# Top-k attention and an MLP mixer in one kernel: q of the first pair split, output sums by two chunks, stores on two queues, and new scheduling weights

## The chip, the core and the metric

The kernel runs on one core of one Trainium2 chip. The core has five engines that run side by side and wait for each other by semaphores: TensorE (PE in the profile; its weight loads are PEld), VectorE (DVE), ScalarE (ACT), GpSimd (POOL) and SyncE (SP, used here to issue DMA transfers). Sixteen DMA engines move data between the chip's memory (HBM) and the on-chip SBUF; TensorE writes its results into PSUM. The metric is the device time of one execution in microseconds, lower is better.

## The reference

Eight batches, eight heads, 576 rows, head dimension 64. For each row of the scores the 32 largest are kept, the others are masked, and the softmax of what is kept weighs v. The heads are put side by side (512 channels) and go through a mixer: an MLP over the rows (576 to 256 to 576) with a residual, then an MLP over the channels (512 to 1536 to 512) with a residual.

```python
scores = scale * np.matmul(q, k.transpose(0, 1, 3, 2))
kth = np.partition(scores, -top_k, axis=-1)[..., -top_k:-top_k + 1]     # top_k = 32
scores = np.where(scores >= kth, scores, -1000000000.0)
attn = np.exp(scores - np.max(scores, axis=-1, keepdims=True))
attn = attn / (np.sum(attn, axis=-1, keepdims=True) + 1e-09)
x = heads_side_by_side(np.matmul(attn, v))                              # [8, 576, 512]
xt = x.transpose(0, 2, 1)
u = x + (np.maximum(xt @ w_tok1, 0.0) @ w_tok2).transpose(0, 2, 1)
out = u + np.maximum(u @ w_ch1, 0.0) @ w_ch2
```

## The kernel before

Work is done in 32 pairs of heads. A pair has nine units of 128 score rows: groups g = 0 to 3 with two units each (one of each head) and g = 4 with one unit, which holds the last 64 rows of both heads. For a unit, TensorE makes the scores, ScalarE copies them to SBUF (`S`, L472), VectorE finds the 8 largest of each of seven segments (L479), and from these an upper threshold `thi`; ScalarE counts and signs what lies above (`sg`, L493), GpSimd multiplies that with the scores (`X`, L496), and VectorE finds the exact threshold `tlo` in the product (L508). Then the masked exponentials `Pm` are made in one of four forms, named by a letter for each g:

```python
FORMS = ("DRADR", "QQADR", "DRQDD", "RQADR")            # by pair % 4
FIRST = ("QRDRD", "RQRQR", "QQRRQ", "DRRQR")            # pairs 0 to 3
LAST = ("DQADA", "AAAAD")                               # pairs 30 and 31
# D: ScalarE exp; GpSimd: nt, Z (one per unit), M, then Pm = E * M
# R: ScalarE makes the mask (L534), TensorE adds it to recomputed scores, ScalarE exp
# Q: as R, but GpSimd makes the mask (nt, Z, M)
# A: ScalarE exp into PSUM (L565), VectorE compares and multiplies (L568)
```

`Pm` is transposed by DMA (in the last pair's g = 3 and 4 by TensorE), and TensorE multiplies it with v; VectorE normalises (L455, L456). After four pairs a batch's mixer follows.

The kernel does not fix the order of instructions by hand. It adds every operation to a plan with an engine, an estimated length and a due time, and a list scheduler in Python puts them in order once: among what can run, the earliest possible start is taken first, and nearly equal starts are settled by the due time. The due times come from a table of weights:

```python
W = dict(T=2.1, ev=-7.1, evh=5.45, seg=10.8, t2=3.2, ct=2.3, xm=3.05, dm=3.5, m5=-3.85, ...)
...
pick = earliest start; within 0.03 us of each other: smallest (due, number)
```

Loading and transposing q and k of a pair (`cp` is a ScalarE copy out of PSUM with a scale):

```python
def ld_q():
    ld_main(qL, q, nc.sync)                       # two DMAs: rows 0 to 511 of each head
    for h in range(2):
        nc.sync.dma_start(out=qL.t[64*h : 64*h+ST, 4, h, :], in_=q[b, h0+h, SM:S, :])
...
lq = plan.add("SP", 0.24, tl, ld_q, acq=[qL], dma=1.4)
lk = plan.add("SP", 0.2, tl + 0.1, ld_kv(kL, k, keng), acq=[kL], dma=1.4)     # keng: ScalarE's queue in pair 0
oq = plan.add("PE", 0.75, tt, tr(pq, qL, 5), [lq], acq=[pq, qT], use=[qL])     # five transposes, L385
ok = plan.add("PE", 0.75, tt + 0.5*T, tr(pk, kL, 4), [lk], acq=[pk, kT], use=[kL])
eq = plan.add("ACT", 0.6, tt + T, cp(qT, pq, 5*P), [oq], use=[pq, qT])         # L395
ek = plan.add("ACT", 0.57, tt + 1.5*T, cp(kT, pk, S), [ok], use=[pk, kT])
...
om = plan.add("PE", 1.3 if g < 4 else 1.2, T*i0, scores ..., [eq, ek], acq=bs + [Ss], use=[qT, kT])   # L414, L406
```

PSUM is four tiles `big` of two halves each; a half alone is a `one`. The last batch has a mixer of its own. Three of its four channel blocks (`NC - 1`) are done ahead, as partial hidden products (L737) that ScalarE copies to SBUF (L749, `ready`). When the last block of UT is there (L658), a loop over the 12 inner chunks `fc` (`NF`) finishes them:

```python
r1 = plan.add("PE", 1.8, d - 0.5, lambda: residual(range(NC - 1)), uts[0 : NC-1] + l4, acq=outs, use=[UT])   # L764; outs: three big
for fc in range(NF):
    for u in range(2):                            # two halves of 288 rows
        pb = Buf("one")
        o = plan.add("PE", 0.16, ..., hidden(... last block ...), uts + [ready[fc]], acq=[pb], ...)          # L737
        adds.append(plan.add("DVE", 0.42, ..., part(fc) = pb + part(fc), [o, ready[fc]], ...))               # L787
    if fc == 0:
        prev = plan.add("PE", 0.4, ..., residual((NC - 1,)), uts + [r1], ...)
    relus.append(plan.add("ACT", 0.57, ..., relu of part(fc) into H2, adds, ...))                             # L792
    if fc < NF - 2:
        def f(fc=fc):
            for t in range(5):
                outer(t, fc)                      # H2 chunk times wc2b into output block t, L769
        prev = plan.add("PE", 1.12, d + 2.0, f, [relus[-1], prev], use=[H2] + outs)
for t in range(5):
    ...                                           # the last two chunks, then the copy out of PSUM (L808)
    plan.add("SP", 0.06, ..., lambda: nc.sync.dma_start(out=out[...], in_=ob...), [e], use=[ob], dma=1.0)     # L811
```

Of the kernel before, what the change touches and what calls it, by code (L numbers as in the profile page):

```python
# [8 lines left out]
P = 128  # L9
# [3 lines left out]
HUP = float(2.0**20)  # L13
# [15 lines left out]
NEG = -float(2.0**120)  # L29
BIG = float(2.0**60)  # L30

# [178 lines left out]
def kernel(  # L210
# [11 lines left out]
    nc = tc.nc  # L222
# [3 lines left out]
    AF = mybir.ActivationFunctionType  # L226
# [10 lines left out]
    SM = 512  # L237
# [81 lines left out]
    for t in qLs:  # L319
        nc.vector.memset(t[:, 4, :, :], 0.0)  # L320
    for t in vLs:
        nc.vector.memset(t[:, 4, :, :], 0.0)
    for t in Xs:
# [13 lines left out]
    def flat(t):  # L337
        return t[:, :, :].rearrange("p j c -> p (j c)")
# [4 lines left out]
    def pair_ops(p):  # L343
# [7 lines left out]
        def ld_main(buf, src, eng):  # L351
            for h in range(2):
# [2 lines left out]
                    in_=src[b, h0 + h, 0:SM, :].rearrange("(p t) d -> p t d", t=4),  # L355
                )

        def ld_q():
            ld_main(qL, q, nc.sync)
            for h in range(2):  # L360
                nc.sync.dma_start(
                    out=qL.t[64 * h : 64 * h + ST, 4, h, :], in_=q[b, h0 + h, SM:S, :]
                )

        def ld_kv(buf, src, eng):
            def f():
# [14 lines left out]
        def tr(dst, src, n):  # L381
            def f():
                o = flat(dst.t)
                for t in range(n):
                    nc.tensor.transpose(o[:, t * P : (t + 1) * P], src.t[:, t, :, :], identF[:, :])  # L385
                if n == 4:
# [7 lines left out]
        def cp(dst, src, n):  # L394
            return lambda: nc.scalar.activation(  # L395
                out=dst.t[:, 0:n], in_=flat(src.t)[:, 0:n], func=AF.Copy, scale=HUP)

        eq = plan.add("ACT", 0.6, tt + T, cp(qT, pq, 5 * P), [oq], use=[pq, qT])
        ek = plan.add("ACT", 0.57, tt + 1.5 * T, cp(kT, pk, S), [ok], use=[pk, kT])
# [20 lines left out]
        for g in range(5):  # L420
            n = 2 if g < 4 else 1
            bs, Ss = [Buf("big") for _ in range(n)], Buf("S")
            i0 = 9 * p + 2 * g
            om = plan.add("PE", 1.3 if g < 4 else 1.2, T * i0, lambda g=g, bs=bs: scores(g, bs, True), [eq, ek], acq=bs + [Ss], use=[qT, kT])
            PT.append(unit_ops(i0, n, bs, Ss, om, p, g, scores, [qT, kT]))


# [286 lines left out]
    def mlp_tail(b, base, UT, H2, uts):  # L714
# [44 lines left out]
        def residual(ccs):  # L759
            for t in range(5):  # L760
                for cc in ccs:

                    w = C if cc == 0 else P
                    nc.tensor.matmul(  # L764
                        out=acc(t, cc * P, cc * P + w), lhsT=UT.t[:, cc, t * P : t * P + rows[t]],
                        rhs=identW[:, 0:w], start=(cc == 0), stop=False, skip_group_check=True)
# [4 lines left out]
                start=False, stop=(fc == NF - 1), skip_group_check=True)  # L771

        d = base + 4 * 1.3
        r1 = plan.add("PE", 1.8, d - 0.5, lambda: residual(range(NC - 1)), uts[0 : NC - 1] + l4, acq=outs, use=[UT])
        relus = []
        prev = None
        for fc in range(NF):
            B_, half = parts[fc]
            d += 1.4
            adds = []  # L780
            for u in range(2):
                pb = Buf("one")
# [4 lines left out]
                adds.append(plan.add("DVE", 0.42, d + 0.3 + 0.4 * u, lambda fc=fc, pb=pb, us=us: nc.vector.tensor_tensor(  # L787
                    out=part(fc)[:, us], in0=pb.t[:, pb.half, 0:HS], in1=part(fc)[:, us], op=ALU.add),
                    [o, ready[fc]], use=[pb, B_]))
            if fc == 0:  # L790
                prev = plan.add("PE", 0.4, d + 0.5, lambda: residual((NC - 1,)), uts + [r1], use=[UT] + outs)
            relus.append(plan.add("ACT", 0.57, d + 1.2, lambda fc=fc: nc.scalar.activation(  # L792
                out=H2.t[:, fc, :], in_=part(fc), func=AF.Relu), adds, use=[B_, H2]))
            if fc < NF - 2:
                def f(fc=fc):
                    for t in range(5):
                        outer(t, fc)

                prev = plan.add("PE", 1.12, d + 2.0, f, [relus[-1], prev], use=[H2] + outs)
        for t in range(5):  # L800
            def f(t=t):
                for fc in (NF - 2, NF - 1):
                    outer(t, fc)

            prev = plan.add("PE", 0.45, d + 2.5 + 0.1 * t, f, [prev] + relus[NF - 2 :], use=[H2] + outs)
# [5 lines left out]
            plan.add("SP", 0.06, d + 4 + 0.1 * t, lambda t=t, ob=ob: nc.sync.dma_start(  # L811
                out=out[b, t * P : t * P + rows[t], :], in_=ob.t[0 : rows[t], t % 2, 0:C]), [e], use=[ob], dma=1.0)


# [59 lines left out]
    c2 = plan.add("PE", 0.2, tc_ + 9, lambda: nc.tensor.matmul(  # L874
        out=pb.t[0:1, 0, 0:1], lhsT=ones[:, :], rhs=bad[:, 3:4], start=True, stop=True), [c1], acq=[pb])
    c3 = plan.add("DVE", 0.15, tc_ + 10, lambda: nc.vector.tensor_copy(out=flag[:, :], in_=pb.t[0:1, 0, 0:1]),
                  [c2], use=[pb], lat=3.0)
    plan.add("SP", 1.0, tc_ + 11, lambda: found.append(
        nc.values_load(flag[0:1, 0:1], min_val=0, max_val=P * (NT + 2))), [c3])
# [181 lines left out]
```

## Time and profile before

| | |
|---|---|
| time, median of 3 runs | 832.36 us (831.48 to 832.98) |
| span of the profiled execution | 830.7 us |
| granted TensorE clock, mean | 0.977 of full speed |
| busiest engine by line | VectorE: L479 404.2 us, L508 220.5 us, L483 98.1 us, L482 97.7 us |
| first scan on VectorE | 12.09 us |
| last store issued | 823.52 us |
| HBM read, written | 35.85 MB, 9.44 MB |

An engine's busy time as a share of the span says how full it is over the whole; a table of windows says when. The chain that ended last is followed back from the last instruction, at each step to what released it; an item on that chain delays the end, one beside it does not. In the timeline an item has its start, its length, engine and line, what it writes and reads, and in brackets the engine's idle time before it and what ended it. Times are in microseconds.

### The profile page before, as it was taken

Reading aid. Unit: us, or ns where it says so; the run is one execution under the profiler, and the core shown is the slowest. Engines: PE = TensorE matmul, PEld = TensorE weight load, DVE = VectorE, ACT = ScalarE, POOL = GpSimd, SP = SyncE. Lnnn points to the kernel's source line nnn. Section 1 sums busy time; section 2 is a strip of 40 time slices with the busy share of each in tenths; the row PEclk is TensorE's granted clock in tenths of the full one; section 3 lists DMA queues with packets and bytes.
Section 4 is the critical chain, followed back from the end, with each engine's and each line's share of the span. In section 5 each row is a group of like instructions: output and inputs, shape, how many; then the busy total and the mean of one; then the engine's idle time right before and its main releaser. Section 6 shows DMA issues by size and latency. Waiting matters only on the chain.

```text
span 830.7 us, 20132 instructions
## 1 busy us (share of the span) xinstructions
PE 735.4 (89%) x5744; PEld 464.6 (56%) x5783; DVE 787.7 (95%) x4794; ACT 753.1 (91%) x1468; POOL 691.4 (83%) x560
## 2 busy tenths in 40 slices
PE   5778778899989989899989999899989999898994
PEld 3445455665556555665556555565556655574641
DVE  5999999999999999999999999999999999999853
ACT  6899998999999999999999999999999999997732
POOL 1999887899899988899988998899989999998400
PEclk9799999999999999999999999999999999999998
DMA  5986955547645565437646466445565385234301
GB/s 128 148 150 118 168 119 99 101 77 155 134 90 96 111 134 113 97 80 147 137 88 115 82 151 117 99 99 122 129 107 109 72 150 126 44 69 92 80 1 61
DMA packets 311064, 89.62 MB, mean 108 GB/s; under 512 B 303776, under 2 KB 305696, under 8 KB 310944
## 3 DMA queue, kind: packets, MB, share of 16 engines
q1 hardware_dynamic: 306992, 84.19, 51.0%
q0 software_dynamic: 2752, 3.77, 3.1%
q8 instruction: 47, 0.77, 0.4%
q14 instruction: 73, 0.60, 0.2%
q10 hardware_dynamic: 1200, 0.30, 0.2%
HBM read 35.85 MB, written 9.44 MB: 55 GB/s over the span
## 4 chain that ended last, share of the span: by engine, by line
DVE 73%; PE 10%; ACT 8%; issue 4%; POOL 2%; DMA 1%; SPq 0%; DVEq 0%; ACTq 0%; POOLq 0%
DVE cd L479 28%; DVE tlo L508 18%; DVE cd L483 9%; DVE m L482 5%; DVE X L504 3%; DVE thi L490 3%; PE big L414 3%; DVE Pm L568 3%; DVE Xb L456 2%; ACT S L472 2%; ACT sg L493 2%; PE big L769 1%; PE big L624 1%; POOL X L496 1%; PE big L737 1%
## 5 line engine op out<-in xcount | busy, mean ns | idle before, releaser
L479 DVE MAX8 cd<-S 128x8 f32<-128x82 f32 (+1 forms) x2016 | 404.2, 231 | 8.9 <-ACT S L472 8.9
L496 POOL TENSOR_TENSOR X<-S,sg 128x1152 f32<-128x1152 f32 (+1 forms) x160 | 343.8, 2161 | 46.2 <-ACT sg L493 45.5
L414 PE MATMUL big<-kT,qT 64*128 64x288 f32 x1504 | 255.4, 439 | 13.0 <-ACT kT L395 11.5
L493 ACT ACTIVATE sg<-S,thi 128x576 bf16<-128x576 f32 x288 | 232.0, 807 | 16.6 <-DVE thi L490 12.0
L508 DVE MAX8 tlo<-X 128x8 f32<-128x588 f32 x288 | 220.5, 766 | 1.4 <-POOL nt L518 0.9
L414 PEld LDWEIGHTS big<-kT,qT 64*128 64x128 f32 x1504 | 151.0, 192 | 83.2 <-issue 21.6
L472 ACT COPY S<-big 128x576 f32<-128x576 f32 x288 | 177.9, 670 | 5.1 <-PE big L414 3.7
L527 POOL TENSOR_TENSOR Pm<-E,M 128x1152 bf16<-128x1152 bf16 (+1 forms) x51 | 112.1, 2198 | 4.3
L669 PE MATMUL big<-UT,wc1b 128*128 128x288 bf16 x672 | 95.1, 286 | 19.7 <-ACT Pm L560 7.7
L689 PE MATMUL big<-wc2b,H 128*128 128x512 bf16 (+1 forms) x399 | 97.9, 379 | 5.7 <-issue 1.9
L483 DVE MATCH_REPLACE8 cd<-m,cd 128x14 f32<-128x14 f32 (+1 forms) x576 | 98.1, 171 | 0.0
L482 DVE MAX8 m<-cd 128x8 f32<-128x14 f32 (+1 forms) x576 | 97.7, 170 | 0.0
L560 ACT ACTIVATE Pm<-big 128x576 bf16<-128x576 f32 x143 | 88.4, 674 | 6.8 <-PE big L414 4.8
L669 PEld LDWEIGHTS <-wc1b 128*128 128x128 bf16 x672 | 63.0, 97 | 53.3 <-issue 37.6
L521 POOL TENSOR_SCALAR Z<-S,nt 128x576 f32<-128x576 f32 x94 | 70.3, 748 | 8.8
L554 PE MATMUL big<-M,sink 128*128 128x288 bf16 x286 | 53.5, 293 | 18.8 <-ACT M L534 5.6
L406 PE MATMUL big<-kT,qT 128*128 128x288 f32 x220 | 66.8, 427 | 3.7 <-ACT S L472 1.4
L689 PEld LDWEIGHTS <-H 128*128 128x128 bf16 (+1 forms) x420 | 39.2, 100 | 50.1 <-issue 13.4
L493 ACT ACTIVATION_READ_ACCUMULATOR sg<-S,thi 128x1 f32 x288 | 64.9, 225 | 0.0
L437 PEld LDWEIGHTS <-PT 128*128 128x128 bf16 x1600 | 52.3, 98 | 14.3 <-issue 9.2
L437 PE MATMUL big<-vb,PT 128*128 128x65 bf16 x1600 | 56.0, 194 | 4.3 <-DMA PT<-Pm 2.5
L534 ACT ACTIVATE M<-S,tlo 128x576 bf16<-128x576 f32 x76 | 56.4, 784 | 2.7 <-DVE tlo L508 2.4
(109 smaller groups left out, 1042.5 us busy)
## 6 DMA issues: line engine op xcount, KB each, us to landing
qL<-in_q_dram SPq DMA_DIRECT2D x64, 128.0 KB, 2.8
vL<-in_v_dram SPq DMA_DIRECT2D x64, 128.0 KB, 2.8
kL<-in_k_dram SPq DMA_DIRECT2D x62, 128.0 KB, 2.8
out_dram<-ob SPq DMA_DIRECT2D x14, 512.0 KB, 3.0
PT<-Pm SPq DMA_TRANSPOSE x158, 3.4
wc1b<-in_moe_w_ch_dram POOLq DMA_DIRECT2D x4, 384.0 KB, 6.1
wc2b<-in_moe_w_ch_dram POOLq DMA_DIRECT2D x4, 384.0 KB, 5.8
qL<-in_q_dram SPq DMA_DIRECT2D x64, 16.0 KB, 2.3
```

Source lines behind the costliest of these rows:

```text
L414: nc.tensor.matmul(out=row(bs[h].t)[:, lo:hi], lhsT=qT.t[r, g * P : (g + 1) * P], rhs=kT.t[r, lo:hi], start=start, stop=True,)
L437: nc.tensor.matmul(out=o[:, g, :], lhsT=src[:, (5 * h if g < 4 else 0) + j, :], rhs=vb.t[:, j, h, :], start=(j == 0), stop=(j == 4),)
L472: evs = [plan.add("ACT", 0.525, t + W["ev"] * T + W["evh"] * h * T, lambda h=h: nc.scalar.copy(out=S_.t[:, h, :], in_=row(s[h].t)), [om], ...
L479: segs = [plan.add("DVE", 0.148, th + W["seg"] * T + 0.01 * a, lambda a=a, cd=cd, h=h: nc.vector.max(cd.t[:, a, :], S_.t[:, h, bounds[a] : ...
L482: m_ = lambda n_, cd=cd, m8=m8: (lambda: nc.vector.max(m8.t[:, :], cd.t[:, :, 0:n_]))
L483: c_ = lambda n_, cd=cd, m8=m8: (lambda: nc.vector.match_replace(cd.t[:, :, 0:n_], m8.t[:, :], cd.t[:, :, 0:n_], NEG))
L493: cts.append(plan.add("ACT", 0.77, th + W["ct"] * T, lambda h=h, i=i, r=r: nc.scalar.activation(out=sg.t[:, h, :], in_=S_.t[:, h, :], func ...
L496: xm = plan.add("POOL", 0.1 + 1.19 * n, te + W["xm"] * T, lambda: nc.gpsimd.tensor_tensor(out=X.t[:, XW - S : XW - S + n * S].rearrange("p ...
L508: m = plan.add("DVE", 0.682, te + W["m5"] * T + 0.3 * h * T, lambda h=h, r=r: nc.vector.max(tlo[:, r : r + 8], X.t[:, h * XW : (h + 1) * X ...
L527: last = [plan.add("POOL", 0.12 + 1.11 * n, te + W["pm"] * T, lambda: nc.gpsimd.tensor_tensor(out=Pm.t[:, 0:n, 0:S], in0=E.t[:, 0:n, :], i ...
L669: nc.tensor.matmul(out=row(pb.t)[:, lo:hi], lhsT=wc1b[:, cc, fc * P : (fc + 1) * P], rhs=UT.t[:, cc, lo:hi], start=(cc == 0), stop=(cc == ...
L689: nc.tensor.matmul(out=pb.t[0:r, pb.half, :], lhsT=H2.t[:, fc, cs], rhs=wc2b[:, fc, :], start=(fc == 0), stop=False)
```

## The change

Four things change in the code, and with them the weights of the plan and the forms of four pairs.

In the first pair the last chunk of q (the rows from 512 on) is loaded, transposed and copied as operations of their own, which only the scores of g = 4 wait for; k is copied out of PSUM by VectorE; the memset of `qL` comes first. In the last mixer the loop's output products are taken for two inner chunks at a time, and the first residual products wait for the partial hidden products. The five last stores alternate between SyncE's and ScalarE's queues. The final check of the kernel takes half a PSUM tile instead of a whole one. It is meant to let the scores start sooner, to leave the scheduler better orders, and to shorten the end.

```diff
 W = dict(
-    T=2.1, ev=-7.1, evh=5.45, seg=10.8, t2=3.2, ct=2.3, xm=3.05, dm=3.5, m5=-3.85, ex=9.2, tn=-1.5,
-    z=5.3, mk=-1.2, pm=-2.7, rw=-3.9, og=7.85, eg=7.95, ea=3.15, st=7.0, tr=-0.45, pv=7.5, fin=-9.5,
-    mlp=11.1, stp=1.35, mlq=13.6, stq=1.2, hp=2.85, hps=5.15,
+    T=2.0, ev=-8.45, evh=7.05, seg=3.9, t2=4.5, ct=1.7, xm=3.35, dm=-8.15, m5=-11.15, ex=11.0,
+    tn=-9.4, z=5.9, mk=-11.4, pm=2.35, rw=-0.8, og=6.5, eg=7.6, ea=2.3, st=7.25, tr=-0.35, pv=1.95,
+    fin=3.55, mlp=10.8, stp=1.35, mlq=22.9, stq=0.55, hp=-1.5, hps=0.0,
 )
-FIRST = ("QRDRD", "RQRQR", "QQRRQ", "DRRQR")
-LAST = ("DQADA", "AAAAD")
+FIRST = ("QRDRD", "RQRQR", "QRRQQ", "RRRQQ")
+LAST = ("DRADD", "DAADA")
...
+    for t in qLs:                                  # moved to the front from further down
+        nc.vector.memset(t[:, 4, :, :], 0.0)
     make_identity(nc, identF[:, :])
...
-        lq = plan.add("SP", 0.24, tl, ld_q, acq=[qL], dma=1.4)
+        first = p == 0
+        lq2 = None
+        if first:
+            lq = plan.add("SP", 0.2, tl, lambda: ld_main(qL, q, nc.sync), acq=[qL], dma=1.4)
+            lq2 = plan.add("SP", 0.2, tl + 0.05, lambda: ld_rest(nc.sync), use=[qL], dma=0.2)
+        else:
+            lq = plan.add("SP", 0.24, tl, ld_q, acq=[qL], dma=1.4)
...
-        oq = plan.add("PE", 0.75, tt, tr(pq, qL, 5), [lq], acq=[pq, qT], use=[qL])
+        oq = plan.add("PE", 0.75, tt, tr(pq, qL, 4 if first else 5, True), [lq], acq=[pq, qT], use=[qL])
...
+        if first:
+            eq = plan.add("ACT", 0.5, tt + T, cp(qT, pq, SM), [oq], use=[pq, qT])
+            ek = plan.add("DVE", 0.67, tt + T, lambda: nc.vector.tensor_scalar(
+                out=kT.t[:, :], in0=flat(pk.t)[:, 0:S], scalar1=HUP, scalar2=None, op0=ALU.mult), [ok], use=[pk, kT])
+            o4 = plan.add("PE", 0.2, tt + T, tr(pq, qL, 5, True, 4), [lq2, oq], use=[qL, pq])
+            eq4 = plan.add("ACT", 0.2, tt + 1.5 * T, cp(qT, pq, 5 * P, SM), [o4], use=[pq, qT])
...
-        r1 = plan.add("PE", 1.8, d - 0.5, lambda: residual(range(NC - 1)), uts[0 : NC - 1] + l4, acq=outs, use=[UT])
+        r1 = plan.add("PE", 1.8, d - 0.5, lambda: residual(range(NC - 1)), uts[0 : NC - 1] + l4 + ready, acq=outs, use=[UT])
...
-            if fc < NF - 2:
+            if fc == 1 or (fc > 1 and fc % 2 and fc < NF - 2):
                 def f(fc=fc):
                     for t in range(5):
-                        outer(t, fc)
-                prev = plan.add("PE", 1.12, d + 2.0, f, [relus[-1], prev], use=[H2] + outs)
+                        for c in (fc - 1, fc):
+                            outer(t, c)
+                prev = plan.add("PE", 2.4, d + 2.0, f, [relus[-2], relus[-1], prev], use=[H2] + outs)
...
-            plan.add("SP", 0.06, d + 4 + 0.1 * t, lambda t=t, ob=ob: nc.sync.dma_start(
+            q_ = nc.sync if t % 2 == 0 else nc.scalar
+            plan.add("SP" if t % 2 == 0 else "ACT", 0.6, d + 4 + 0.1 * t, lambda t=t, ob=ob, q_=q_: q_.dma_start(
...
-    pb = Buf("big")                                # the final check's PSUM
+    pb = Buf("one")
```

More of the change, by code (lines that the diff above doesn't have):

```diff
@@ L318 @@
         nc.vector.memset(kdum[:, j : j + 1], float(2 * (j + 1) - 529))
-    for t in qLs:
-        nc.vector.memset(t[:, 4, :, :], 0.0)
     for t in vLs:
@@ L356, in ld_main, with ld_rest @@
                 )
+        def ld_rest(eng):
+            for h in range(2):
+                eng.dma_start(
+                    out=qL.t[64 * h : 64 * h + ST, 4, h, :], in_=q[b, h0 + h, SM:S, :]
+                )
         def ld_q():
             ld_main(qL, q, nc.sync)
[L360 to L363, printed above, removed]
+            ld_rest(nc.sync)
         def ld_kv(buf, src, eng):
@@ L379, in pair_ops, with tr @@
         pq, pk = Buf("big"), Buf("big")
-        def tr(dst, src, n):
+        def tr(dst, src, n, isq=False, lo=0):
             def f():
                 o = flat(dst.t)
-                for t in range(n):
+                for t in range(lo, n):
                     nc.tensor.transpose(o[:, t * P : (t + 1) * P], src.t[:, t, :, :], identF[:, :])
-                if n == 4:
+                if not isq:
                     nc.tensor.transpose(o[:, SM:S], src.t[0:ST, 4, :, :], identF[0:ST, 0:ST])
@@ L390, in pair_ops, with cp @@
         tt = t0 - W["tr"] * T
[L391 removed]
+        oq = plan.add("PE", 0.75, tt, tr(pq, qL, 4 if first else 5, True), [lq], acq=[pq, qT], use=[qL])
         ok = plan.add("PE", 0.75, tt + 0.5 * T, tr(pk, kL, 4), [lk], acq=[pk, kT], use=[kL])
[L394 removed]
+        def cp(dst, src, n, lo=0):
             return lambda: nc.scalar.activation(
[L396 to L399 removed]
+                out=dst.t[:, lo:n], in_=flat(src.t)[:, lo:n], func=AF.Copy, scale=HUP)
+        eq4 = None
+        if first:
[4 more added lines that the diff above has]
+            eq4 = plan.add("ACT", 0.2, tt + 1.5 * T, cp(qT, pq, 5 * P, SM), [o4], use=[pq, qT])
+        else:
+            eq = plan.add("ACT", 0.6, tt + T, cp(qT, pq, 5 * P), [oq], use=[pq, qT])
+            ek = plan.add("ACT", 0.57, tt + 1.5 * T, cp(kT, pk, S), [ok], use=[pk, kT])
         ov = plan.add("ACT", 0.6, t0 + 4 * T, lambda: nc.scalar.copy(
@@ L423, in pair_ops @@
             i0 = 9 * p + 2 * g
-            om = plan.add("PE", 1.3 if g < 4 else 1.2, T * i0, lambda g=g, bs=bs: scores(g, bs, True), [eq, ek], acq=bs + [Ss], use=[qT, kT])
+            om = plan.add("PE", 1.3 if g < 4 else 1.2, T * i0, lambda g=g, bs=bs: scores(g, bs, True), [eq, ek] + ([eq4] if g == 4 else []),
+                          acq=bs + [Ss], use=[qT, kT])
             PT.append(unit_ops(i0, n, bs, Ss, om, p, g, scores, [qT, kT]))
@@ L874 @@
     c2 = plan.add("PE", 0.2, tc_ + 9, lambda: nc.tensor.matmul(
-        out=pb.t[0:1, 0, 0:1], lhsT=ones[:, :], rhs=bad[:, 3:4], start=True, stop=True), [c1], acq=[pb])
-    c3 = plan.add("DVE", 0.15, tc_ + 10, lambda: nc.vector.tensor_copy(out=flag[:, :], in_=pb.t[0:1, 0, 0:1]),
+        out=pb.t[0:1, pb.half, 0:1], lhsT=ones[:, :], rhs=bad[:, 3:4], start=True, stop=True), [c1], acq=[pb])
+    c3 = plan.add("DVE", 0.15, tc_ + 10, lambda: nc.vector.tensor_copy(out=flag[:, :], in_=pb.t[0:1, pb.half, 0:1]),
                   [c2], use=[pb], lat=3.0)
```

## The prediction

> **What bounds the kernel now.** I read, in this order: the page's busy shares, the table of windows, the chain of waits at the start, the timeline of the last 50 us, and the last stores. First, which engine is full, on the page:
>
> ```profile
> PE 735.4 (89%) x5744; PEld 464.6 (56%) x5783; DVE 787.7 (95%) x4794; ACT 753.1 (91%) x1468; POOL 691.4 (83%) x560
> ```
>
> VectorE (DVE) is busy 787.7 of 830.7 us. Its 43 idle us are not spread out. The table of windows (us of the stretch, then busy time of each engine, granted clock, DMA share, GB/s) shows where they lie:
>
> ```profile
> 0.00:12.10 12.10, 6.39 (x31) 4.86 (x31) 2.02 (x29) 4.02 (x6) 0.70 (x6) 1.00 0.56 127
> 200.00:400.00 200.00, 186.61 (x1463) 118.17 (x1472) 199.15 (x1231) 192.01 (x376) 182.93 (x147) 1.00 0.57 114
> ...
> 790.00:819.00 29.00, 25.39 (x135) 10.65 (x136) 14.89 (x39) 11.12 (x18) 0.00 (x0) 0.94 0.00 1
> 819.00:831.00 12.00, 1.73 (x8) 0.47 (x6) 1.99 (x3) 1.17 (x2) 0.00 (x0) 0.68 0.31 106
> ```
>
> In the middle VectorE lacks 0.85 us in 200. The idle time is 10.1 us ahead of the first scan, 14.1 us in the last MLP, 10.0 us in the stores and the end. The windows from 12.1 to 710 us together hold only about 4 us of it, the one from 710 to 790 about 5 us. So new priorities can win at most some 4 us in the long middle; the rest must come from the two ends or from less VectorE work.
>
> The chain at the start (start, length, what):
>
> ```profile
> 1.50 4.08 DMA qL<-in_q_dram
> 5.71 2.15 PE big L385 x9
> 8.16 1.26 PE big L385 x5
> 9.42 2.02 PE big L414 x8
> ...
> 12.09 1.27 DVE cd L479 x8
> ```
>
> The q transfer that released TensorE was issued at 1.50, which is the second main piece, not the last chunk (those issues start at 2.40). Nine transposes follow, one more for k, then five for the next pair at 8.16, which stand in TensorE's order before the first scores.
>
> The end, from the timeline (start, length, engine, line, output<-input, idle before):
>
> ```profile
> 784.65 0.19 POOL L518 TENSOR_SCALAR nt<-tlo 128x1 f32<-128x1 f32 x1 [1.87 <-DVE tlo L508]
> 786.52 1.28 POOL L527 TENSOR_TENSOR Pm<-E,M 128x576 bf16<-128x576 bf16 x1
> 789.95 0.82 DVE L456 TENSOR_TENSOR Xb<-big,rd 128x640 bf16<-128x640 f32 x1
> 793.43 1.93 PE L764 MATMUL big<-identW,UT 128*128 128x512 bf16 x15
> 793.54 0.64 ACT L658 CAST UT<-big 128x576 bf16<-128x576 f32 x1 [0.44 <-PE big L652]
> ...
> 808.26 1.37 PE L769 MATMUL big<-wc2b,H 128*128 128x512 bf16 x5
> 809.56 0.42 PE L737 MATMUL big<-UT,wc1b 128*128 128x288 bf16 x2
> 810.02 0.82 DVE L787 TENSOR_TENSOR E<-big,E 128x288 f32<-128x288 f32 x2 [1.04 <-PE big L737]
> 810.93 0.68 ACT L792 ACTIVATE H<-E 128x576 bf16<-128x576 f32 x1 [1.18 <-DVE E L787]
> 811.67 1.37 PE L769 MATMUL big<-wc2b,H 128*128 128x512 bf16 x5
> ```
>
> The last attention unit has form D: its mask runs on GpSimd (POOL) for 3.15 us, 784.65 to 787.80, while VectorE mostly waits. Then come the last MLP and its loop over 12 inner chunks: hidden product, two additions, ReLU, five output products. The loop takes 3.41 us for two chunks (808.26 to 811.67): it is a closed round of waits, 2.11 us from a hidden product to its output product and 1.30 us of output products.
>
> [...] The trace has 0.692 us for 512 columns[...], so I take 0.76 us for the k copy. [...] the seven at 818.50 took 1.70 us, 243 ns each[...] and I use 243.
>
> **Part 1, the start.** Splitting q frees the first four transposes from the last chunk, but the main piece landed last by the chain, so this gives at most 0.1 us. By the kernel's scheduling rule (earliest possible start first) the fifth q transpose still goes ahead of k's, because in its model q's remainder lands before k. So k is transposed at 8.17 as before. ScalarE stood idle for 0.45 us just before its k copy (0.65 us), so VectorE's 0.76 us copy wins nothing by itself. Moving the memset of qL up spends 0.3 us that VectorE has free. The next pair's five transposes (1.26 us) may or may not still stand ahead of the scores; kT is ready near 8.9 and the scores start at 9.4, so 0.5 us is at stake. I count **0.2 us less**.
>
> **Part 2, other forms for early and late pairs.** An A unit costs VectorE one operation of 805 ns (40.4 us for 51). The late pairs go from 3 + 8 A units to 2 + 5: four fewer, 4 x 0.805 = 3.2 us less VectorE work. The early pairs have no A in either version. A D unit instead costs POOL about 0.10 + 0.75 + 0.58 + 1.19 = 2.6 us (half of 193, 1147 and 2369 ns, and 748). The late pairs go from five D units to nine: 10.5 us more, less 2.8 us for one Q pair that becomes R. POOL was idle 6.23 + 4.63 + 1.87 = 12.7 us in 766 to 785, so it has room. The very last unit becomes A: 0.85 us of VectorE in place of 3.15 us of POOL. But the unit pair before it becomes D, with 0.19 + 1.5 + 1.15 + 2.37 = 5.2 us, with 0.2 us of hops, after its thresholds. These were known at 783.2 before; earlier by 3.4 us (parts 1 and 2) they are known near 779.8, so that chain ends near 785.2; ten transposes (0.8), a copy (0.82), PV (0.5) and norm (1.1) add 3.2 us: 788.4 against 790.8. **2.4 us less** remains of 3.2.
>
> **Part 3, the order in the last MLP.** The residual products (L764, 1.93 us) now wait for all partial hidden products, whose priority is lower and equal. Before, they ran from 793.43 to 795.29 and held up the first hidden product, though the last UT copy ended at 794.18. If they now run while VectorE normalises, 1.1 us goes: **1.0 us less**. Taking two chunks at a time makes ten output products, 10 x 0.243 = 2.43 us in one piece, and removes no product. Only one PSUM buffer (two halves) is left for the hidden products. By the same rule I read the order as: output of two chunks, then the second half of the next odd chunk, addition, ReLU, output. That round is 2.43 + 1.69 = 4.12 us for two chunks, more than 3.41. But it starts with output products about 2.9 us after the first hidden product, has four such rounds, and ends at 2.9 + 4 x 4.12 + 2.43 + 1.7 = 23.5 us, against 818.50 - 795.29 = 23.2 before, since the loop before lost time in its first chunks. **0.3 us more.**
>
> **Part 4, the stores.**
>
> ```profile
> L811 SPq DMA_DIRECT2D out_dram<-ob x4: 356/394/613, 820.1 to 821.9; - x4
> L811 SPq DMA_DIRECT2D out_dram<-Z x1: 482/482/482, 823.5 to 823.5; - x1
> ```
>
> The fifth store was issued at 823.52, though its copy ended at 821.53 and the fourth issue at about 822.3; the first store's landing, up to 3.4 us after 820.07, fits that wait. With three stores on one queue and two on the other it can issue near 821.7. The data keep the DMA engines busy until about 824.5 either way. I take **1.7 us less** of the 1.8 at most.
>
> **Part 5, all priorities.** T and 26 weights change the order on all engines over 700 us. At most about 4 us are to be won; ScalarE and TensorE are so full that an unlucky order loses as much. I take **0.3 us less** with 2 us either way.
>
> Sum: -0.2 - 2.4 - 1.0 + 0.3 - 1.7 - 0.3 = -5.3; 832.36 - 5.3 = **827.0 us**.
>
> **Rivals.** (a) POOL becomes the bound at the end: pairs 30 and 31 then hold 18 units of scaling (about 1.2 us each) and nine D units, 45 us in two pairs that take about 49. For it: POOL was 90% busy from 12 to 740 us and its operations stay in order. Against it: the idle 12.7 us. It would give back the 2.4 us and perhaps 2 more: 829 to 832. (b) The two-chunk loop runs at 4.12 us in every round and loses the good start: 3 to 4 us more, 830 to 831. Or the other way: if both halves of the next odd chunk stand ahead of the output products, ReLU hides behind them and the round falls to about 3.0 us: 2 to 4 us less, 823 to 825. (c) The new priorities make a recurring bubble in the middle, such as a wait of 0.5 us per pair: 31 x 0.5 = 15 us more. Nothing in the change points to one, but no view of the old trace can exclude it; a search over the weights that kept the better ones speaks against it.
>
> **Range and chances.** The independent parts spread by about 2 us (end), 2 us (loop), 2 us (middle) and 1 us (start and stores): together about 3.7, so 8 in 10 gives 821.5 to 832.5. Two per cent is 16.6 us; faster by that would need almost half of all idle time of VectorE, slower by that needs (c). I give 0.02 and 0.02, and 0.96 to within 2%.
>
> **What would show it.** First scan at 11.5 to 12.1; VectorE's form A at 47 instead of 51, its busy total near 785; last norm ending near 788; no residual products between the last UT copy and the first hidden product; about 4.1 us from one ten-product group to the next; last store issued within 1 us of its copy. Wrong if the stretch from 12 to 780 us changes by over 2 us, if POOL has no idle time in the last pairs, or if the loop's round is near 3.0 us.

## The result, and the profile after

The changed kernel takes 838.36 us, median of four runs (836.39 to 840.53), against 832.67 us (831.48 to 833.45) for the kernel before beside it: a ratio of 1.007 with a 95% interval of 1.0041 to 1.01. It is about 5.7 us slower. The prediction was 827.0 us with a range that ended at 832.5: the sign was wrong and the time lies above the range. The profiled execution is the shortest of the four, with a span of 834.6 us against 830.7 before, so the two traces show 3.9 us of the 5.7.

The busy shares of the page say that the engines' work came out much as expected:

```profile
PE 739.3 (89%) x5756; PEld 465.6 (56%) x5795; DVE 785.7 (94%) x4791; ACT 754.0 (90%) x1470; POOL 695.0 (83%) x564
```

VectorE does 2.0 us less work than before (785.7 against 787.7) and the span is longer: the loss is waiting time. The table of windows of the changed kernel, with the same columns as before (us of the stretch, busy time of PE, PEld, DVE, ACT, POOL, granted clock, DMA share, GB/s), shows where:

```profile
0.00:12.10 12.10, 6.26 (x29) 4.87 (x31) 2.78 (x29) 3.11 (x5) 0.70 (x6) 1.00 0.56 125
200.00:400.00 200.00, 188.31 (x1466) 118.20 (x1474) 199.46 (x1227) 191.76 (x377) 182.72 (x147) 1.00 0.59 113
790.00:819.00 29.00, 20.56 (x110) 9.09 (x111) 13.11 (x34) 9.19 (x15) 0.00 (x0) 0.94 0.00 1
819.00:834.00 15.00, 5.14 (x23) 1.93 (x23) 3.28 (x7) 2.54 (x4) 0.00 (x0) 0.89 0.25 84
```

At the start nothing changed in size. From 200 to 400 us VectorE is busier by 0.3 us; from 12.1 to 200 us, not in the table, it is less busy by 1.3 us (184.44 of 187.90 us against 185.74). From 790 to 819 TensorE is busy 20.6 us where it was 25.4, and 5.1 us of its work has slid into the last window, where it had 1.7. The last MLP has become slower, and the marks of the two profiled executions put a number on it:

| us from the start | before | after |
|---|---|---|
| first scan on VectorE | 12.09 | 12.41 |
| last norm ends | 790.77 | 789.84 |
| last UT copy ends | 794.18 | 793.25 |
| first hidden product of the loop | 795.29 | 794.37 |
| output products of the last two chunks start | 818.50 | 823.53 |
| last store issued | 823.52 | 826.98 |
| span | 830.7 | 834.6 |

The loop over the inner chunks takes 823.53 - 794.37 = 29.2 us where it took 23.2: **6.0 us more**. The stretch before it is 0.9 us shorter and the end after it (834.6 - 823.53 = 11.1 against 12.2) 1.1 us shorter. That is the whole difference of the traces: 6.0 - 0.9 - 1.1 = 4.0, which is the 3.9 us but for rounding.

How the loop loses it stands in its timeline (start, length, engine and line, output<-input, idle time before and what ended it):

```profile
799.22 3.84 PE L788 MATMUL big<-wc2b,H 128*128 128x512 bf16 x10
802.99 0.60 PE L756 MATMUL big<-UT,wc1b 128*128 128x288 bf16 x2
803.63 0.46 DVE L806 TENSOR_TENSOR qL<-big,qL 128x288 f32<-128x288 f32 x1 [3.76 <-PE big L756]
804.01 0.45 DVE L806 TENSOR_TENSOR kL<-big,kL 128x288 f32<-128x288 f32 x1
...
804.51 0.28 PE L756 MATMUL big<-UT,wc1b 128*128 128x288 bf16 x1 [0.91 <-DVE kL L806]
804.83 0.46 DVE L806 TENSOR_TENSOR kL<-big,kL 128x288 f32<-128x288 f32 x1 [0.37 <-PE big L756]
805.34 0.28 PE L756 MATMUL big<-UT,wc1b 128*128 128x288 bf16 x1 [0.55 <-DVE kL L806]
...
810.11 2.44 PE L788 MATMUL big<-wc2b,H 128*128 128x512 bf16 x10
...
814.77 2.44 PE L788 MATMUL big<-wc2b,H 128*128 128x512 bf16 x10
```

From one group of ten output products to the next it is 814.77 - 810.11 = 4.66 us. Four hidden halves (L756) stand between two groups. The first two run together. The third, at 804.51, waits 0.91 us and the fourth, at 805.34, 0.55 us, each for VectorE. The additions that read them end at 804.09 and 804.46; the third product needs one half only, but starts 0.05 us after the second of these, and the fourth again 0.05 us after the latest addition (804.83 + 0.46 = 805.29), not after the one that freed its own half. So each of these two starts only after the addition of the half before it, and a half costs 0.83 us (805.34 - 804.51). Meanwhile ScalarE and VectorE have almost nothing to do during the ten products: VectorE's idle time before 803.63 is 3.76 us.

### The profile page after: what moved, and what is told of

It reads as the page before. It is cut to its first block, busy times and chain, and to the rows that moved or that the text cites. A ratio compares the mean times of both kernels' runs of the same rounds, so it can differ in the third digit from the quotient of the medians.

```text
span 834.6 us, 20146 instructions
## 1 busy us (share of the span) xinstructions
PE 739.3 (89%) x5756; PEld 465.6 (56%) x5795; DVE 785.7 (94%) x4791; ACT 754.0 (90%) x1470; POOL 695.0 (83%) x564
## 4 chain that ended last, share of the span: by engine, by line
DVE 80%; PE 7%; ACT 5%; issue 3%; DMA 2%; POOL 1%; SPq 0%; DVEq 0%; ACTq 0%; POOLq 0%
DVE cd L498 31%; DVE tlo L527 20%; DVE cd L502 10%; DVE m L501 5%; DVE X L523 4%; DVE thi L509 4%; DVE Pm L587 3%; DVE Xb L475 2%; PE big L788 2%; PE big L432 2%; ACT sg L512 1%; PE big L756 1%; DMA PT<-Pm 1%; ACT M L553 1%; ACT S L491 1%
## 5 line engine op out<-in xcount | busy, mean ns | idle before, releaser
L432 PE MATMUL big<-kT,qT 64*128 64x288 f32 x1512 | 259.9, 438 | 13.1 <-ACT kT L404 9.6
L546 POOL TENSOR_TENSOR Pm<-E,M 128x1152 bf16<-128x1152 bf16 (+1 forms) x52 | 114.4, 2199 | 3.8
L573 PE MATMUL big<-M,sink 128*128 128x288 bf16 x290 | 55.4, 297 | 17.3 <-ACT M L553 7.3
L553 ACT ACTIVATE M<-S,tlo 128x576 bf16<-128x576 f32 x79 | 59.4, 783 | 2.5 <-DVE tlo L527 2.3
L543 POOL TENSOR_SCALAR M<-Z 128x1152 bf16<-128x1152 f32 (+1 forms) x52 | 55.8, 1072 | 4.5
L535 ACT ACTIVATE E<-S 128x1152 bf16<-128x1152 f32 (+1 forms) x52 | 59.0, 1135 | 0.2
```

The lines of the kernel that those rows point to most:

```text
L432: nc.tensor.matmul(out=row(bs[h].t)[:, lo:hi], lhsT=qT.t[r, g * P : (g + 1) * P], rhs=kT.t[r, lo:hi], start=start, stop=True,)
L546: last = [plan.add("POOL", 0.12 + 1.11 * n, te + W["pm"] * T, lambda: nc.gpsimd.tensor_tensor(out=Pm.t[:, 0:n, 0:S], in0=E.t[:, 0:n, :], i ...
```

## The experiments

Two theories after the result. **Theory L (loop):** the two-chunk loop costs 6 us by itself, because large pieces and few PSUM halves leave the additions unhidden. **Rival M (middle):** the new weights and forms lose time in the order, and the loop only shows the delay. The first four runs try parts of the change alone.

### The change with the loop set back (a_single)

```diff
-            if fc == 1 or (fc > 1 and fc % 2 and fc < NF - 2):      # output products of two chunks
+            if fc < NF - 2:                                         # of one chunk, as before
...
-                        for c in (fc - 1, fc):
-                            outer(t, c)
+                        outer(t, fc)
```

> The changed kernel with only the loop of the last mixer set back: five output products after each single chunk. Theory (the two-chunk loop costs the loss: its round takes 4.65 us for two chunks against 3.41, and it is 29.2 us long against 23.2): the loop falls back to about 23 us, the time to about 838.4 - 6 = 832.4 us or, by the profiled span, 834.6 - 6 + 1.7 = 830 us; below the kernel before. Rival (the new order in the first 790 us, or stalls of it that only some executions show, cost the loss): it stays at 837 to 839 us.

Measured: 833.06 us (827.86 to 837.00), ratio to the kernel before 1.0002 (0.9983 to 1.0022). Its loop takes 23.2 us again (799.27 to 822.49). Without the loop the loss is gone, so the loop is the loss. But nothing of the 5.6 us that the prediction gave to the other parts shows either: together they come to 0.02%, by the interval between 1.4 us won and 1.8 us lost.

### The two-chunk loop alone (b_pairs)

The kernel before, with the loop's output products taken as in the change and nothing else.

> The kernel before with only the two-chunk loop put in. Theory: about 832.7 + 6 = 838.5 us, the round 4.65 us[...]. Rival (the loop is no worse by itself, only with the new weights): 832 to 834 us.

Measured: 839.93 us (836.96 to 840.81), ratio 1.0075 (1.0055 to 1.0096); its loop runs from 796.44 to 825.23, 28.8 us, with 816.59 - 811.93 = 4.66 us from one group of ten to the next. Alone it costs what the whole change costs. Theory L holds from both sides; M falls as the explanation of the slowdown, and remains as a question of why the rest wins nothing.

### The stores alone (b_queues)

```diff
-            plan.add("SP", 0.06, ..., lambda ...: nc.sync.dma_start(
+            q_ = nc.sync if t % 2 == 0 else nc.scalar
+            plan.add("SP" if t % 2 == 0 else "ACT", 0.6, ..., lambda ...: q_.dma_start(
```

> The kernel before with only the five last stores put on two queues. Theory (the last store stood behind the load of the check's flag into a register of SyncE, not behind a full queue; but on two queues the scheduler places that load again between two stores of SyncE): from the start of the last output products to the last store's issue 3.4 us as in the changed kernel in place of 5.0, so about 1.6 us less: 831.1 us. Rival (what was saved there came from elsewhere): 832.5 us, the same.

Measured: 831.53 us (828.01 to 834.46), ratio 0.9985 (0.9974 to 0.9996): 1.2 us won (0.3 to 2.2 by the interval), where 1.7 was predicted. From the last output products to the last store it is 822.81 - 818.37 = 4.4 us, against 5.0.

### Was it the full queue, or the flag? (b_flag)

The prediction blamed the late fifth store on a queue that was full. The traces suggest another cause: SyncE also loads the flag of the kernel's final check into a register (L879), in order among the stores. This run moves that load behind the fifth store and leaves the queue as it was.

```diff
-        nc.values_load(flag[0:1, 0:1], ...)), [c3])
+        nc.values_load(flag[0:1, 0:1], ...)), [c3] + stores)
```

> The kernel before, stores on one queue, but the load of the check's flag into SyncE's register stands after the fifth store. Theory (the load made the fifth store late): the fifth store is issued at about 822.3 in place of 823.5, right after the fourth, and the time falls by about 1.2 us to 831.5, unless the load then sets the end itself. Rival (the queue of one engine is full, as the prediction put it): the fifth store is still issued near 823.5 and the time stays at 832.7.

Measured: 833.18 us (829.24 to 837.98), ratio 1.0004 (0.9988 to 1.0019). The timeline of SyncE's queue, for the kernel before and then for this experiment:

```profile
820.07 2.20 SPq L811 DMA_DIRECT2D out_dram<-ob  x4
823.52 0.48 SPq L811 DMA_DIRECT2D out_dram<-Z  x1
```

```profile
820.38 2.72 SPq L812 DMA_DIRECT2D out_dram<-ob  x4
823.19 0.48 SPq L812 DMA_DIRECT2D out_dram<-Z  x1
```

Before, the fifth store went out 1.25 us after the end of the fourth issue (822.27), with the load between them; here it went out 0.09 us after it (823.10), on a single queue. So the load was what held it, and not a full queue. The expected 822.3 was missed all the same, since the first four issues took 2.72 us instead of 2.20: from the output products to the fifth store it is 823.19 - 818.80 = 4.4 us instead of 5.0. And the time is no better: that store then landed after 4.1 us rather than 3.0, the load took longer in its new place, and from the output products to the end of the span it is 13.3 us in this trace against 12.2 before. The row of the load in the queue (shortest, median and longest in ns) for the kernel before:

```profile
L879 SPq TENSOR_LOAD <-flag x1: 750/750/750, 822.3 to 822.3; - x1
```

and for the kernel of this experiment:

```profile
L880 SPq TENSOR_LOAD <-flag x1: 1365/1365/1365, 823.7 to 823.7; - x1
```

So the load explains the late issue, and the earlier issue of that one store wins nothing here.

### Loads of the last MLP's weights: later, earlier, between (as_spread, b_load, as_loadT)

In a_single's trace one stretch stood out: from 60 to 110 us VectorE was busy 45.30 of 50 us (49.27 in the kernel before), and two DMA transposes of `Pm`, one after the other from 79.34 us, took 13.95 us of the chain. There the four 384 KB loads of `wc2b` for the last MLP fall, whose due times depend on the weight `T`, which the change set from 2.1 to 2.0. They were moved in a_single in two ways, and the due times that T = 2.0 gives them were put alone into the kernel before:

```diff
     l4 = [plan.add("POOL", 0.7, (26 + 4 * j) * T, load_wc(wc2b, ...), ...) for j in range(4)]
 # as_spread (on a_single): (28 + 7 * j) * 2.1
 # b_load (on the kernel before): (26 + 4 * j) * 2.0
 # as_loadT (on a_single): (26 + 4 * j) * 2.1
```

> The changed kernel with the loop set back (as in a_single) and the four loads of wc2b given due times further apart, (28 + 7j) x 2.1 us of the plan in place of (26 + 4j) x T. In a_single and in the changed kernel three of these loads are issued within 5 us (75.7 to 80.4 us), VectorE is short of work from 90 to 105 us and a transpose by DMA takes up to 11 us to land. Theory (loads that crowd together hold up the transposes, and this took back what the rest of the change won): VectorE loses 2 to 4 us less between 60 and 140 us and the time is about 830 us against 833.1 for a_single. Rival (the stall belongs to the new order of the transposes and would come with any placing of the loads): 832 to 834 us, VectorE's busy time from 60 to 140 us as in a_single.

> The kernel before with the due times of the four wc2b loads alone set as T = 2.0 sets them. The last three then stand in GpSimd's order as in the changed kernel, close together. Theory: the stall between 80 and 110 us appears here too and the time rises by 1 to 4 us, to 833.5 to 836. Rival (the loads matter only together with the new order): 832 to 833 us.

> a_single with the due times of the wc2b loads as the kernel before has them (T = 2.1 for these alone): only the fourth load moves back in GpSimd's order, by some seven rows. Theory of the crowded loads: three of the four are still close, so the stall of a_single between 80 and 110 us (3.5 us of VectorE's time) shrinks but does not go: 831 to 833 us against 833.1. Rival (no effect of the loads, only of the order around them): 833 us or more.

b_load: 834.30 us (831.71 to 836.86), ratio 1.0018 (1.0007 to 1.0029). Windows of the kernel before, and then of b_load:

```profile
80.00:110.00 30.00, 23.15 (x176) 15.13 (x177) 29.54 (x188) 29.22 (x60) 25.15 (x23) 0.94 0.87 151
```

```profile
80.00:110.00 30.00, 21.66 (x156) 14.12 (x156) 26.60 (x162) 25.81 (x52) 22.86 (x21) 0.84 0.85 146
```

VectorE loses 2.9 us in this stretch. The slowest transpose of `Pm` took 8.1 us from issue to landing instead of 6.8, while the medians stayed at 3.4. The last two loads were issued together at 82.28, right behind one at 80.18; before, the last came 5 us later. The loads' due times alone cost the kernel before 0.18%, 1.5 us. That makes them a likely part of the reason why the rest of the change wins nothing; in the changed kernel itself neither of the next two runs shows it. And new due times for the loads move other operations too (as_spread shows it), so that crowded loads slow the transposes is the likely cause of the 1.5 us, not shown by itself.

as_spread: 835.67 us (833.98 to 840.32), ratio 1.0035 (1.0022 to 1.0048). Its expectation failed. The stall itself was gone (VectorE busy 29.81 of 30 us from 80 to 110, against 26.47 in a_single), but moving four loads moved the order of everything after: from 200 to 700 us VectorE was busy 496.74 us, in a_single 498.98. It won 3.3 us at one place and lost 2.2 at another; from 12.1 to 60 us it lost 1.6 more (46.17 against 47.76), and the last UT copy ended 4.9 us after the norm instead of 3.4. Here the order could not be mended at one place and kept at the others.

as_loadT: 832.46 us (830.51 to 834.74), ratio 0.9995 (0.9979 to 1.001). Against a_single's 833.06 it is 0.6 us in the right direction and inside both intervals: inconclusive.

### A loop that hides its waits (a_best, b_best)

If theory L is right, small output pieces behind the *next* hidden product should hide the addition and ReLU. Both kernels make a chunk's two hidden halves in one piece, add them in one instruction of 576 columns, and place the output products of chunk n-2 behind the hidden product of chunk n. The residual products wait for the last UT copy and stand behind the first hidden product.

```diff
+            pb = Buf("big")                                   # both halves at once
+            o = plan.add("PE", 0.42, d, hid, uts + [ready[fc]] + ([prev] if fc > 2 else []), acq=[pb], ...)
+            a = plan.add("DVE", 0.75, ..., tensor_tensor over [128, 2, 288], [o, ready[fc]], ...)
...
-            if fc < NF - 2:                                   # after ReLU of this chunk: its output products
+            if fc >= 2:
+                prev = products(fc - 2, [o])                  # after this hidden product: those of two chunks ago
```

a_best is the changed kernel with this loop and as_spread's loads. b_best is the kernel before (its weights, forms and loads) with this loop and the stores on two queues.

> The changed kernel with the loads spread as in as_spread and a loop of another shape: one hidden product and one addition for a whole chunk, and the output products of a chunk placed behind the hidden product of the chunk two further on; the residual products stand behind the first hidden product. Theory (the loop is a round of waits, so an order in which ReLU and addition run beside other output products is bound by TensorE alone): a round of two chunks takes 2 x (5 x 0.243 + 2 x 0.14) = 3.0 us against 3.41 before and 4.65 in the change, the loop about 19 to 20 us against 23.2, and the time 3 to 4 us under as_spread: 826 to 828 us. Rival (VectorE's addition or the clock sets the pace): round at 3.4 us or more, 829 us or more.

> The kernel before with the same loop as a_best and the stores on two queues, its own weights, forms and loads. Theory: 832.2 less 1.2 (stores) less 3 to 4 (loop): 827 to 828.5 us. If the new weights and forms are worth something once the loads are spread, a_best is faster than this by 1 to 2 us; if not, the two are equal.

a_best: 831.22 us (829.41 to 832.57), ratio 0.9984 (0.9975 to 0.9993); 4.4 us below as_spread, which has the same loads, but above the 826 to 828 us expected, since as_spread itself had come out at 835.67 and not near 830. b_best: **827.33 us** (825.95 to 829.40), ratio 0.9937 (0.9912 to 0.9962): faster than both kernels. The new weights, forms and start thus win nothing with this loop and these loads either: with them it is 3.9 us slower than without. From 200 to 700 us VectorE was busy 496.76 us in a_best, as in as_spread, and 498.39 in b_best.

The timeline of b_best:

```profile
804.86 0.42 PE L737 MATMUL big<-UT,wc1b 128*128 128x288 bf16 x2
805.12 1.36 PE L769 MATMUL big<-wc2b,H 128*128 128x512 bf16 x5
805.32 0.76 DVE L798 TENSOR_TENSOR E<-big,E 128x576 f32<-128x576 f32 x1 [0.79 <-PE big L737]
...
812.72 2.62 PE L769 MATMUL big<-wc2b,H 128*128 128x512 bf16 x10
813.10 1.19 PEld L769 LDWEIGHTS <-H 128*128 128x128 bf16 x7 [0.29 <-ACT H L801]
```

Of the last ten output products one goes ahead at 812.72; the others follow the last ReLU at 813.10, which is the mark used above (before, too, one goes ahead, at 817.84). So the loop takes 813.10 - 793.27 = 19.8 us, 3.4 less than before, and the first hidden product follows the last UT copy (793.22) after 0.05 us instead of 1.1. The two are 4.5 of the 5.3 us won. In the loop, the group before began at 803.57, this one at 805.12: 1.55 us per chunk, 3.1 us for two, with no wait on TensorE. The addition and ReLU run beside the five products.

### The same loop with ten products in one piece (b_lag2)

Is it the size of the piece or the lag that matters? This is b_best with the output products of two chunks in one piece.

```diff
-            if fc >= 2:
+            if fc >= 3 and fc % 2:
                 prev = products(fc - 2, [o])                  # now: for c in (fc - 3, fc - 2)
```

> b_best with one edit: output products for two chunks in one piece of ten, placed behind the hidden product of the chunk two further on. Theory (with one PSUM tile left, each hidden product must wait for the addition of the one before; single pieces of output products fill that wait once per chunk, a double piece only once per two chunks): a round of two chunks takes about 2.4 (ten products) + 0.3 + 1.3 (addition and back) + 0.3, less overlap: 3.8 to 4.1 us against 3.0 in b_best, five such rounds, the time 4 to 5 us above b_best: 831 to 832 us. Rival (only the order of the changed kernel is at fault, not the double piece): the round stays at 3.0 us and the time at 827.3.

Measured: 832.52 us (830.46 to 835.09), ratio 0.9998 (0.9982 to 1.0014), 5.2 us above b_best. The timeline of b_lag2:

```profile
804.48 0.42 PE L737 MATMUL big<-UT,wc1b 128*128 128x288 bf16 x2
805.75 0.41 PE L737 MATMUL big<-UT,wc1b 128*128 128x288 bf16 x2 [0.85 <-DVE E L799]
805.99 2.44 PE L769 MATMUL big<-wc2b,H 128*128 128x512 bf16 x10
```

The next group starts at 809.94: 3.95 us for two chunks against b_best's 3.1. With two hidden products in a row and one tile for them, the second waits 0.85 us for the addition, with nothing of TensorE's in between. With one tile left for the hidden products, the size of the piece is the cause, also in a loop that lags.

### The other forms of the late pairs (b_last)

```diff
-LAST = ("DQADA", "AAAAD")
+LAST = ("DRADD", "DAADA")
```

on b_best. The prediction gave this 2.4 us.

> b_best with the changed kernel's forms for pairs 30 and 31 alone (four A units fewer, four D units more, the last unit A). The prediction's step: VectorE's busy time 3.2 us lower, the last norm 2.4 us earlier, the time 825 us. Rival (POOL's D chain of the unit pair before the last, and the partial hidden products that stand ahead of the last product with v in TensorE's order, take it back): the norm at most 1 us earlier or later, 826.5 to 829 us.

Measured: 827.64 us (825.03 to 828.65), ratio 0.9934 (0.9907 to 0.9960), beside b_best's 827.33: nothing won. VectorE's busy time did fall by 2.5 us (786.4 to 783.9). The timeline of b_last tells where it went:

```profile
784.43 0.49 DVE L583 COPY PT<-big 128x640 bf16<-128x640 bf16 x1 [2.05 <-PE big L579]
786.94 0.82 DVE L583 COPY PT<-big 128x1280 bf16<-128x1280 bf16 x1 [2.02 <-PE big L579]
789.91 0.22 DVE L455 RECIPROCAL rd<-big 128x10 f32<-128x10 f32 x1 [2.14 <-PE big L437]
```

The same three places in b_best:

```profile
785.20 0.82 DVE L583 COPY PT<-big 128x1280 bf16<-128x1280 bf16 x1 [0.88 <-PE big L579]
787.45 0.49 DVE L583 COPY PT<-big 128x640 bf16<-128x640 bf16 x1 [1.43 <-PE big L579]
788.73 0.22 DVE L455 RECIPROCAL rd<-big 128x10 f32<-128x10 f32 x1 [0.79 <-PE big L437]
```

VectorE is done with its last mask 1.95 us earlier (782.37 against 784.32), but then waits 2.05 + 2.02 + 2.14 = 6.2 us in the last pair instead of 3.1: less work for an engine that then waits is no gain. The second of these waits is for GpSimd's mask chain, which ends at 786.12, the third for the products with v (PV), which stand behind eighteen partial hidden products (786.74 to 789.10) in TensorE's order: the rival. The last norm ends at 790.99, in b_best at 789.82, though b_last's first scan was 1.25 us earlier.

## Why the prediction was wrong, step by step

**The step that failed is part 3's loop.** As put: "By the same rule I read the order as: output of two chunks, then the second half of the next odd chunk, addition, ReLU, output. That round is 2.43 + 1.69 = 4.12 us for two chunks, more than 3.41. But it starts with output products about 2.9 us after the first hidden product ... **0.3 us more.**" It measured 6.0 us more. The order that I took for the round, and with it the overlap, was wrong; three terms of the sum were too small:

- *The start.* 799.22 - 794.37 = 4.85 us, not 2.9 (before: 798.48 - 795.29 = 3.2). I let the halves before the first group follow one another freely. They go one at a time, 0.83 us each (796.60, 797.43, 798.26, 799.09 in the trace): 1.9 us.
- *The order.* I took one half to stand between two groups. There are four; the last two of them wait. A steady round is 4.65 us, not 4.12: 0.5 us in each of four rounds.
- *The clock.* While the halves trickled in, TensorE was busy 1.47 of the 3 us from 797 to 800. The ten products after it took 3.84 us, with a granted clock of 0.50 from 800 to 803 us; ten products in a later round took 2.44 us (810.11), with a granted clock of 1.00 from 810.2 to 812.4. The window of the changed kernel:

```profile
800.00:803.00 3.00, 3.00 (x9) 0.65 (x7) 0.00 (x0) 0.00 (x0) 0.00 (x0) 0.50 0.00 0
```

What sets the clock is not shown. The kernel before had 0.52 in the same 3 us, so this is no loss against it; but its 23.2 us hold that loss, and my sum, which I set beside them, did not.

With order and clock the four rounds take 819.42 - 799.22 = 20.2 us instead of 16.5: 2.1 us by the order, 1.6 by the slow first round.

1.9 + 3.7 = 5.6 us of the 5.7 by which the step was off. Rival (b) named this ("runs at 4.12 us in every round and loses the good start: 3 to 4 us more") and was the right one, but undersized. Its other half, the round in which ReLU is hidden, came true under another order: with the additions hidden, b_best's round is 3.1 us, where I had written "about 3.0 us".

**Part 1, 0.2 us: nothing.** The copy of k took 0.76 us, which was my estimate (the trace of before has 0.692 us for VectorE's copies of 512 columns, L808), and was no limit, as argued. What was at stake, the next pair's five transposes, did not move. These lines are of the changed kernel's start:

```profile
5.84 1.30 PE L394 MATMUL big<-identF,qL 128*128 128x128 f32 x5 [5.84 <-DMA qL<-in_q_dram]
8.22 1.33 PE L394 MATMUL big<-identF,qL 128*128 128x128 f32 x5
8.33 0.76 DVE L411 TENSOR_SCALAR kT<-big 128x576 f32<-128x576 f32 x1 [5.46 <-PE big L396]
9.48 3.20 PE L432 MATMUL big<-kT,qT 64*128 64x288 f32 x16
```

TensorE still waits for q until 5.84 us, and the five transposes at 8.22 still stand ahead of the scores, which start at 9.48 (before: 9.42). Over the runs with a profile the first scan began at 11.95 us in the mean with the old start (eight of them, 11.13 to 12.46) and 12.11 with the new (five, 11.63 to 12.41).

**Part 2, 2.4 us less: right in its work, wrong in its worth.** VectorE's mask operations of form A went from 51 to 47 and VectorE's total to 785.7, as said (47, "near 785"). The mask chain of the last D unit also ended as said: 782.60 + 2.37 = 784.97, predicted 785.2. What failed is the sum after it. The timeline of the changed kernel:

```profile
782.60 2.37 POOL L546 TENSOR_TENSOR Pm<-E,M 128x1152 bf16<-128x1152 bf16 x1
785.60 2.52 PE L756 MATMUL big<-UT,wc1b 128*128 128x288 bf16 x18
785.87 0.82 DVE L602 COPY PT<-big 128x1280 bf16<-128x1280 bf16 x1 [3.58 <-PE big L598]
787.95 0.78 PE L456 MATMUL big<-vb,PT 128*128 128x65 bf16 x20
...
792.50 1.93 PE L783 MATMUL big<-identW,UT 128*128 128x512 bf16 x15
792.61 0.64 ACT L677 CAST UT<-big 128x576 bf16<-128x576 f32 x1 [0.44 <-PE big L671]
794.37 0.42 PE L756 MATMUL big<-UT,wc1b 128*128 128x288 bf16 x2
```

Eighteen partial hidden products stand in TensorE's order before PV. The copy ends at 786.69 and PV starts only near 787.9, and the 20 products take 0.78 us, not 0.5, so the norm ends at 789.84 rather than 788.4: 0.9 us won in this execution. The sum had no such wait in it. b_last, over its runs, found no gain at all.

**Part 3's other half, 1.0 us less: nothing.** The residual products were to run while VectorE normalises. They can't: what they now wait for, the copy of the last partial product, ends at 792.17, and the norm ends at 789.84. They keep their old place in TensorE's order, right behind the products of the last UT block (792.50 here, 793.43 before), and run up to the first hidden product at 794.37, again 1.1 us after the last UT copy at 793.25. In b_best they stand behind the first hidden product, which then starts 0.05 us after the UT copy.

**Part 4, 1.7 us less: 1.2 in b_queues, 1.1 in the two traces.** The size was near, but the cause I gave, a queue waiting for a landing, was wrong, so that was luck; b_flag shows the register load. Why the two queues gain time and the moved load none isn't settled.

**Part 5, 0.3 us less: not seen.** From 200 to 700 us VectorE is busier by 0.5 us (498.99 against 498.46), while from 12.1 to 200 us it is less busy by 1.3, and b_load shows 1.5 us lost by the due times of four loads. The rest of the weights was tried only together with the other parts, in a_single. Of the 5.6 us that was expected of all parts but the loop, the terms above account for 0.2 + 1.5 + 1.0 + 0.6 + 1.8 = 5.1, an estimate that mixes single traces with the 1.5 us that b_load measured in the kernel before.

**Open.** The trace of a_single has its last norm at 794.75 us and that of the changed kernel, with the same plan up to there, at 789.84. So single traces of one order differ by some us before the tail: 3.8 of these 4.9 us are time that VectorE spent idle between 60 and 200 us (busy 133.12 us in a_single's trace, 136.89 in the other). What is read from one trace there, such as b_load's 2.9 us, is no firmer than that. Why the changed kernel's runs spread over 836.4 to 840.5 isn't settled. Two separate PSUM tiles for the hidden halves, which would test the wait for the other half by itself, were not tried, nor crowded loads with the order of everything else kept.

## What to carry to other kernels

Before merging an engine's work into larger pieces, write down that engine's real order for one round and name what fills each wait; a larger piece that removes no instruction saved nothing here, and it took away what stood between a product and its consumer. Lag hid the wait: the same products, placed behind the hidden product of two chunks on, made the loop 19.8 us instead of 23.2, and doubling the piece there cost 5.2 us. Work taken off the busiest engine counts only where that engine is what the others wait for; look at its idle lines in that stage before adding up its savings.

## What the runs showed of the hardware that was not expected

- A product into one half of a PSUM tile started 0.05 us after the addition that read the *other* half, 0.42 us after its own was free (804.51 against 804.09). The profile puts the wait down to that latest addition; whether the program or the hardware sets it is not shown.
- After about 3 us in which TensorE was half busy (1.47 of 3 us, no pause over 0.6 us), its granted clock was 0.50 for 3 us, in the middle of a kernel whose mean is near 0.98; b_best, which keeps it busy (6.10 of 7 us from 796 to 803), kept 1.00 there, and so did b_lag2, busy 2.15 of 3 us from 797 to 800.
- Loading one word into a SyncE register took 0.75 us between stores in the kernel before, 0.51 us between stores in the changed kernel, and 1.37 us in b_flag, where it stood behind all stores of the queue.
- DMA transposes that land in 3.4 to 3.6 us (median of a run, 60 to 120 us) took up to 8.1 us in b_load, 9.1 us in the changed kernel and 11.0 us in a_single, in the stretch in which the 384 KB loads came close together, and up to 6.8 us in the kernel before.
